# Attention masks added in PSUM by TensorE instead of multiplied in by VectorE, with exp writing the attention tiles and VectorE copying the selected v

## The chip, the core and the metric

The kernel runs on one core of one Trainium2 chip. The metric is the device time of one execution in microseconds. Lower is better. Engines are named as in the profile: PE is TensorE's matmul, PEld its weight load, DVE is VectorE, ACT is ScalarE, POOL is GpSimd and SP is SyncE; L315 is line 315 of the kernel before.

## What is computed

Dilated and plain sliding-window attention (8 batches, 8 heads, 576 positions, head size 64), then a soft mixture of experts over all 4608 rows. The reference, cut to what matters:

```python
def _attn_ref(q, k, v):
    scores = scale * np.matmul(q, k.transpose(0, 1, 3, 2))
    rel = pos[:, None] - pos[None, :]
    mask_plain = (rel >= 0) & (rel < 32)
    mask_dil = (rel >= 0) & (rel < 128) & (rel % 4 == 0)
    masks = np.stack([mask_plain if h < H // 2 else mask_dil for h in range(H)], axis=0)
    scores = np.where(masks[None], scores, -1000000000.0)
    attn = np.exp(scores - np.max(scores, axis=-1, keepdims=True))
    attn = attn / (np.sum(attn, axis=-1, keepdims=True) + 1e-09)
    return np.matmul(attn, v).astype(np.float32)

def _moe_ref(x, phi, w1, w2):       # x: 4608 x 512, 32 slots, 8 experts of 512 -> 1024 -> 512
    logits = x @ phi
    d = softmax of logits over the rows;  slot_input = d.T @ x
    slot_out[e] = np.maximum(slot_input[e] @ w1[e], 0) @ w2[e]
    c = softmax of logits over the slots; return c @ slot_out
```

## The kernel before

A *unit* is one pair of heads of one batch: 32 units, four to a batch, in the order plain, dilated, plain, dilated (`unit`). Heads 0 to 3 are plain and heads 4 to 7 dilated. For each unit the kernel does these stages:

- `transposes`: q and k, loaded with positions on the partitions, are transposed by PE into a ring of two PSUM buffers (L275 for plain heads, L290 for dilated ones), and copied out to qT and kT (ACT at L280; for dilated heads ACT copies q and DVE copies k at L295).
- `scores`: PE multiplies kT by qT (L315). Only blocks of 128 keys against the 160 queries that can see them are computed. A unit has two score tiles (`part` 0 and 1) of two PSUM banks each, one bank for each head. The two heads sit in rows 0 to 63 and 64 to 127 of the array, so each score matmul fills 64 rows. The pool `ps_s`, with the tag `s`, holds two such tiles.
- `softmax_parts`: ACT takes exp of a score tile into fp16 scratch (`pr` at L332, `pd` at L344), and DVE multiplies by a 0/1 mask into the attention tiles: `Pp` for plain heads (L335, three instructions for each unit), `P1` and `P2` for dilated ones (L353, L360). No maximum is subtracted.
- `values`: PE multiplies the attention tiles by v with a column of ones (L395). In a plain unit a block of 128 queries takes a matmul of its own keys and one with the keys of the block before; `Pp` is padded to 256 columns and so all 18 matmuls have 128 output rows. In a dilated unit there are eight such matmuls and sixteen with 32 output rows for the last 16 positions of each residue. DVE takes the reciprocal of the sums and scales (L399, L400).
- `x_transposes` (L416) turns the result for the logits; `front_logits`, `front_rows` and `front_slots` do the softmax over rows and the slot sums of a batch.

v needs a selection for plain heads: `select_v` multiplies v by 0/1 matrices on PE (L205, L216, L225) into two tiles of `ps_s` and one of the ring, once for each batch. ACT copies the three results to `vp` (L213, L234).

The loop at the end of attention emits, for unit u: the scores of u+1, the values of u, the exp and mask of u+1, the transposes of u+3, and parts of the front of the batch before. A scheduler orders the instructions of PE, DVE and ACT from that; POOL's instructions, which are the loads, keep the written order. Each engine executes its list in order and waits by semaphores.

Eight buffers `home0` to `home7` hold first the q, k and v of batch b and later the weights of expert b. POOL issues all loads of q, k and v first, then for each expert w1 (L239) and w2 (L250), where w1 of expert e waits until the transposes of batch e have read home e. After attention, `last_early` and `last_slots` finish the slots of the last batch, `siT` (L654) is made, the experts run in pairs (`expert_in`, L675; `expert_out`, L699), `so` is copied out (L716), and the output phase multiplies (L735), scales on ACT and DVE (L739, L741) and writes (L745, L747).

Of the kernel before, what the change touches and what calls it, by code (L numbers as in the profile page):

```python
# [18 lines left out]
D = 64  # L19
# [17 lines left out]
DW = CL + 16  # L37
OUT_TILES = [(0, 2), (256, 2)] + [(512 + 512 * i, 4) for i in range(7)] + [(4096, 2), (4352, 2)]
# [18 lines left out]
def kernel(  # L57
# [17 lines left out]
    mask = consts.tile([128, QW + 2 * N_SLOTS + 256], FP16, name="mask")  # L75
# [7 lines left out]
    nc.sync.dma_start(out=mask[:, 0 : QW + 64], in_=band_dram.ap())  # L83
# [40 lines left out]
    nc.vector.memset(Pp[:, :, :, QW:], 0.0)  # L124

    nc.vector.memset(Pp[:, :, 4, 64:QW], 0.0)
    nc.vector.memset(Pp[0:1, :, 4, 64:128], 1.0)
    nc.vector.memset(P2, 0.0)
    nc.vector.memset(P2[0:1, :, :, 0, 16:32], 1.0)
    for i in range(2):  # L130
        nc.vector.memset(vd[i][:, :, D : D + 1], 1.0)
# [6 lines left out]
    raw_pool = ctx.enter_context(tc.tile_pool(name="praw", bufs=2))  # L138
    small = ctx.enter_context(tc.tile_pool(name="small", bufs=2))
    x_pool = ctx.enter_context(tc.tile_pool(name="x", bufs=2))  # L140
    dil_pool = ctx.enter_context(tc.tile_pool(name="draw", bufs=2))
# [158 lines left out]
    def scores(u):  # L300
        b, hp = unit(u)
        qT, kT = qTs[u], kTs[u]
        tiles = []
        for part in range(2):
            st = ps_s.tile([128, 2, 512], FP32, name=f"s{u}_{part}", tag="s")
            if hp < 2:
                todo = [(160 * i, 128 * i, 128 * i, QW) for i in range(3)] if part == 0 else [
                    (0, 384, 384, QW), (QW, 512, 512, 64)]
            else:
                todo = [(DW * cc, CL * (2 * cc + part), CL * (2 * cc + part), CL) for cc in range(2)]  # L310
                todo += [(DW * cc + CL, None, CL * (2 * cc + part) + 128, 16) for cc in range(2)]
            for at, k0, q0, n in todo:
                for g in range(2):
                    ks = q0 - 32 * g - 64 * (at // DW) if k0 is None else k0
                    nc.tensor.matmul(  # L315
                        st[:, g, at : at + n],
                        kT[64 * g : 64 * g + 64, ks : ks + 128],
                        qT[64 * g : 64 * g + 64, q0 : q0 + n],
                        start=True,
                        stop=True,  # L320
                    )
            tiles.append(st)
        return tiles

    def softmax_parts(u, tiles):
        b, hp = unit(u)
        for part in range(2):
            st = tiles[part]
            if hp < 2:
                n = (480, 224)[part]  # L330
                pr = raw_pool.tile([128, 2, n], FP16, name=f"pr{u}_{part}", tag=f"pr{part}")
                nc.scalar.activation(out=pr, in_=st[:, :, 0:n], func=AF.Exp, scale=SCALE)  # L332
                for b0, nb, w in ((0, 3, QW),) if part == 0 else ((3, 1, QW), (4, 1, 64)):
                    at = (b0 - 3 * part) * QW
                    nc.vector.tensor_tensor(  # L335
                        out=Pp[:, :, b0 : b0 + nb, 0:w],
                        in0=pr[:, :, at : at + nb * w].rearrange("p h (t c) -> p h t c", c=w),
                        in1=mask[:, None, None, 0:w].broadcast_to([128, 2, nb, w]),
                        op=ALU.mult,
                    )  # L340
                continue
            if part == 0:
                pr = dil_pool.tile([128, 2, 2, 2, DW], FP16, name=f"pd{u}", tag="pd")
            nc.scalar.activation(  # L344
                out=pr[:, part].rearrange("p c e t -> p e c t"),
                in_=st[:, :, 0 : 2 * DW].rearrange("p e (c t) -> p e c t", c=2),
                func=AF.Exp,
                scale=SCALE,
            )
        if hp < 2:  # L350
            return
        pr = pr.rearrange("p a c e t -> p a (c e) t")
        nc.vector.tensor_tensor(  # L353
            out=P1.rearrange("p a c t -> p (a c) t"),
            in0=pr[:, :, :, 0:128].rearrange("p a c t -> p (a c) t"),
            in1=mask[:, None, 0:128].broadcast_to([128, 8, 128]),
            op=ALU.mult,
        )

        nc.vector.tensor_tensor(  # L360
            out=P2.rearrange("p a c s t -> p (a c) s t")[:, :, :, 0:16],
            in0=pr[:, :, :, 128:DW].rearrange("p a c (s t) -> p (a c) s t", s=2),
            in1=mask[:, QW + 64 :].rearrange("p (c s t) -> p c s t", c=8, s=2),
            op=ALU.mult,
        )

    def values(u):
# [7 lines left out]
        for half in range(2):  # L375
# [3 lines left out]
            mms = []  # L379
            for i, blk in enumerate(blocks):  # L380
                for h in range(2):
                    if plain:
                        P, vt = Pp, vp[b % NV]
# [3 lines left out]
                    elif blk < 4:  # L387
                        mms.append((ot[:, i, h], P1[:, h, blk, :], vd[b % 2][:, 4 * (hl + h) + blk, :]))
                    else:
                        for s in range(2):  # L390
                            for c in range(4):
                                vt = vp[b % NV][:, 5, hl + h] if s else vd[b % 2][:, 4 * (hl + h) + c]
                                mms.append((ot[32 * c : 32 * c + 32, i, h], P2[:, h, c, s], vt))
# [109 lines left out]
    def last_early(last):  # L503
# [4 lines left out]
        for dc in range(4):  # L508
# [10 lines left out]
            lr[:, 8:10].rearrange("p i s -> p (i s)"), ident, mask[:, QW : QW + 64],  # L519
# [44 lines left out]
    def spread_masks():  # L564
        sides = mask[:, QW + 64 :].rearrange("p (a c s t) -> p a c s t", a=2, c=4, s=2)
        nc.vector.tensor_copy(
            out=sides[:, :, :, 0].rearrange("p a c t -> p (a c) t"),
            in_=mask[:, None, 128:CL].broadcast_to([128, 8, 16]),
        )
        nc.vector.tensor_copy(  # L570
            out=sides[:, :, :, 1],
            in_=mask[:, QW : QW + 64].rearrange("p (c t) -> p c t", c=4)[:, None].broadcast_to([128, 2, 4, 16]),
        )
        shut = mask[:, QW : QW + 64]
# [206 lines left out]
```

## Time and profile before

| what | value |
|---|---|
| median of 3 runs | 185.55 us (184.9 to 186.19) |
| span of the profiled execution | 183.5 us; no time of its own outside the span is given |
| mean granted TensorE clock over the span | 0.932 |
| PE, PEld busy | 151.8 us (83%), 105.8 us (58%) |
| DVE, ACT, POOL busy | 117.1 us (64%), 115.5 us (63%), 46.9 us (26%) |
| HBM read and written | 62.02 MB, 9.44 MB |
| queue of POOL's loads (q0) | 30.79 MB, 93.9% of 16 DMA engines |
| mask products on DVE (L335, L353, L360) | 16.4 us x48, 10.8 us x16, 4.5 us x16 |
| copies of selected v on ACT (L213, L234) | 9.4 us x16, 4.7 us x8 |
| score matmuls on PE (L315) | 128 of 160 columns, 32 of 64, 128 of 144, 128 of 16 |

The span runs from the first instruction to the last. Busy shares are averages over stages with different limits: attention fills the first 145 us, the experts follow to 157 us, and then the output is written. A wait given for an engine names what came last by the semaphores. Ends of matmuls are modelled, so a busy PE is not a PE at its peak; start-to-start distances are measured.

### The profile page before, as it was taken

Reading aid. Unit: us, or ns where it says so; the run is one execution under the profiler, and the core shown is the slowest. Engines: PE = TensorE matmul, PEld = TensorE weight load, DVE = VectorE, ACT = ScalarE, POOL = GpSimd, SP = SyncE. Lnnn points to the kernel's source line nnn. Section 1 sums busy time; section 2 is a strip of 40 time slices with the busy share of each in tenths; the row PEclk is TensorE's granted clock in tenths of the full one; section 3 lists DMA queues with packets and bytes.
Section 4 is the critical chain, followed back from the end, with each engine's and each line's share of the span. In section 5 each row is a group of like instructions: output and inputs, shape, how many; then the busy total and the mean of one; then the engine's idle time right before and its main releaser. Section 6 shows DMA issues by size and latency. Waiting matters only on the chain.

```text
span 183.5 us, 6054 instructions
## 1 busy us (share of the span) xinstructions
PE 151.8 (83%) x2595; PEld 105.8 (58%) x2595; DVE 117.1 (64%) x363; ACT 115.5 (63%) x208; POOL 46.9 (26%) x77
## 2 busy tenths in 40 slices
PE   1869999999988989998997998898979998885300
PEld 1637776677676667666765767666768644432000
DVE  7605886388877877878779687786970111496410
ACT  2248845689599789779878959977703022675410
POOL 7752555464554654401102001003100000000000
PEclk9999999999999999999999999999995589998555
DMA  5999999999999999999999999999999995199996
GB/s 103 183 203 203 202 203 201 202 202 204 204 201 201 204 199 204 226 211 221 212 216 216 212 216 216 218 212 218 218 214 220 212 208 105 75 440 427 427 427 262
DMA packets 23978, 41.06 MB, mean 224 GB/s; under 512 B 1680, under 2 KB 20240, under 8 KB 21136
## 3 DMA queue, kind: packets, MB, share of 16 engines
q0 software_dynamic: 21584, 30.79, 93.9%
q1 hardware_dynamic: 2368, 9.89, 13.4%
q8 instruction: 20, 0.33, 0.6%
q14 instruction: 6, 0.05, 0.1%
HBM read 62.02 MB, written 9.44 MB: 389 GB/s over the span
## 4 chain that ended last, share of the span: by engine, by line
DMA 74%; issue 15%; POOL 3%; ACT 2%; DVE 1%; PE 0%; POOLq 0%; DVEq 0%; SPq 0%
DMA home<-in_moe_w_dram 31%; DMA home<-in_v_dram 15%; DMA home<-in_k_dram 12%; DMA home<-in_q_dram 9%; DMA out_dram<-ot 7%; ACT ot L739 2%; DVE ot L741 1%; POOL home L250 1%; POOL home L162 1%; POOL home L239 1%; POOL home L184 0%; POOL home L187 0%; ACT so L716 0%; PE sop L699 0%; PE f L735 0%
## 5 line engine op out<-in xcount | busy, mean ns | idle before, releaser
L400 DVE TENSOR_TENSOR x<-o,rc 128x384 f16<-128x384 f32 x64 | 29.9, 482 | 0.5
L332 ACT ACTIVATE pr<-s 128x960 f16<-128x960 f32 (+1 forms) x32 | 24.7, 780 | 1.8 <-PE s L315 1.8
L344 ACT ACTIVATE pd<-s 128x640 f16<-128x640 f32 x32 | 20.9, 706 | 1.7 <-PE s L315 1.7
L162 POOL DMA_DIRECT2D home<-in_v_dram x24 | 16.6, 692 | 16.6 <-DMA home<-in_k_dram 11.6
L205 PE MATMUL sel<-home,pick 32*128 32x256 f16 x128 | 17.8, 307 | 1.4 <-DMA home<-in_v_dram 1.1
L399 DVE RECIPROCAL rc<-o 128x6 f32<-128x6 f32 x64 | 10.2, 177 | 13.5 <-PE o L395 13.4
L416 PE MATMUL rgx<-ident,x 128*128 128x128 f16 x160 | 15.6, 233 | 3.0 <-ACT qT L295 3.0
L741 DVE TENSOR_SCALAR ot<-f,rrow 128x512 f32<-128x512 f32 (+1 forms) x19 | 12.5, 716 | 7.7 <-DMA out_dram<-ot 5.2
L335 DVE TENSOR_TENSOR Pp<-pr,mask 128x960 f16<-128x960 f16 (+2 forms) x48 | 16.4, 394 | 0.4 <-ACT pr L332 0.4
L280 ACT COPY qT<-rgq 128x576 f16<-128x576 f16 x16 | 10.3, 641 | 9.0 <-PE rgq L275 8.5
L422 ACT COPY xT<-rgx 128x512 f16<-128x512 f16 x16 | 9.6, 601 | 10.0 <-PE rgx L416 10.0
L739 ACT ACTIVATE ot<-f,rrow 128x512 f32<-128x512 f32 (+1 forms) x19 | 11.2, 675 | 7.0 <-DMA out_dram<-ot 6.6
L239 POOL DMA_DIRECT2D home<-in_moe_w_dram x8 | 4.3, 534 | 44.4 <-PE rgq L290 36.5
L213 ACT CAST vp<-sel 128x512 f16<-128x512 f32 x16 | 9.4, 590 | 9.2 <-PE sel L205 9.0
L416 PEld LDWEIGHTS <-x 128*128 128x128 f16 x160 | 10.2, 102 | 7.2 <-issue 5.4
L735 PE MATMUL f<-so,ET 128*128 128x512 f16 (+1 forms) x38 | 11.0, 402 | 3.9 <-ACT ot L739 3.0
L275 PEld LDWEIGHTS <-home 96*64 96x64 f16 x384 | 11.9, 123 | 3.9 <-issue 2.0
L184 POOL DMA_DIRECT2D home<-in_k_dram x16 | 10.6, 661 | 10.1 <-DMA home<-in_q_dram 8.2
L395 PE MATMUL o<-vp,Pp 128*128 128x65 f16 x288 | 12.9, 203 | 0.0
L436 PE MATMUL l<-xT,phi 128*128 128x288 f16 x64 | 10.8, 304 | 2.0 <-ACT qT L280 1.7
L295 DVE COPY kTd<-rgk 128x576 f16<-128x576 f16 x16 | 12.0, 752 | 0.6 <-PE rgk L290 0.5
L295 ACT COPY qT<-rgq 128x576 f16<-128x576 f16 x16 | 10.3, 646 | 3.1 <-PE rgq L290 2.6
(105 smaller groups left out, 292.9 us busy)
## 6 DMA issues: line engine op xcount, KB each, us to landing
home<-in_moe_w_dram POOLq DMA_DIRECT2D x15, 1024.0 KB, 30.1
out_dram<-ot SPq DMA_DIRECT2D x7, 1024.0 KB, 7.5
home<-in_k_dram POOLq DMA_DIRECT2D x16, 288.0 KB, 9.9
home<-in_q_dram POOLq DMA_DIRECT2D x15, 288.0 KB, 9.7
home<-in_v_dram POOLq DMA_DIRECT2D x16, 256.0 KB, 9.8
out_dram<-ot SPq DMA_DIRECT2D x3, 512.0 KB, 6.5
home<-in_moe_w_dram POOLq DMA_DIRECT2D x2, 512.0 KB, 27.3
home<-in_v_dram POOLq DMA_DIRECT2D x8, 64.0 KB, 8.9
```

The costliest lines, as they stand in the source:

```text
L162: nc.gpsimd.dma_start(out=dst, in_=v[b, h0 : h0 + n_h, r0 : r0 + 4 * n_p, :].rearrange("h (p r) d -> p h (r d)", r=4),)
L205: nc.tensor.matmul(sel[:, n, 0], pick[rows, r].rearrange("p i j -> p (i j)"), raw[rows, :, r, :], start=(r == 0), stop=(r == 3), tile_posi ...
L275: nc.tensor.transpose(rg[64 * h : 64 * h + 64, r, :], raw[:, 2 * hp + h, D * r : D * r + D], ident[0:NP, 0:NP],)
L295: (nc.scalar.copy if nm == "q" else nc.vector.tensor_copy)(out=dst[:, 0:S].rearrange("c (g p a) -> c g p a", g=4, a=3), in_=rg.rearrange(" ...
L332: nc.scalar.activation(out=pr, in_=st[:, :, 0:n], func=AF.Exp, scale=SCALE)
L335: nc.vector.tensor_tensor(out=Pp[:, :, b0 : b0 + nb, 0:w], in0=pr[:, :, at : at + nb * w].rearrange("p h (t c) -> p h t c", c=w), in1=mask ...
L344: nc.scalar.activation(out=pr[:, part].rearrange("p c e t -> p e c t"), in_=st[:, :, 0 : 2 * DW].rearrange("p e (c t) -> p e c t", c=2), f ...
L395: nc.tensor.matmul(to, lhs, rhs, start=(n == 0), stop=(n == len(mms) - 1), skip_group_check=True)
L400: nc.vector.tensor_tensor(out=x[:, blocks[0] : blocks[0] + nb, D * hl : D * hl + 2 * D].rearrange("p t (h d) -> p t h d", h=2), in0=ot[:, ...
L416: nc.tensor.transpose(rg[:, 128 * blk : 128 * blk + 128], x[:, blk, hl : hl + 128], ident)
L739: nc.scalar.activation(out=ot[:, j, d0:d1], in_=fp, func=AF.Copy, scale=scale)
L741: nc.vector.tensor_scalar(out=ot[:, j, d0:d1], in0=fp, scalar1=scale, scalar2=None, op0=ALU.mult)
```

## The change

The mask becomes a number that is added. `constants` gives 0 where a key may be seen and -60000 where not. For each score tile and head, PE first multiplies the identity by the mask into PSUM (`start=True`), and the scores are added on top (`start=False`). ACT's exp then writes straight into the attention tiles, of which there are now two of each kind (`Pp`, `Pd`), used in turn. The scratch tiles, the mask products on DVE and the zero padding of `Pp` go. In `values`, a plain block's matmul with the keys of the block before now has 32 output rows instead of 128, and the order in each half is first the matmuls with 128 output rows, then those with 32. The sixteen short matmuls of a dilated unit, which went through four residues with one operand and then with the other, take both operands of a residue in turn. The three copies of the selected v move from ACT to DVE. The tile `shut`, used once for the last batch, gets its own buffer, and `spread_masks` spreads the dilated mask into `mask_d`.

The diff, cut to its core:

```diff
-    keep = ((d >= 0) & (d < WINDOW)).astype(np.float16)
+    keep = (d >= 0) & (d < WINDOW)
...
-    band = np.concatenate([keep, ends], axis=1).astype(np.float16)
+    band = np.where(np.concatenate([keep, ends], axis=1), 0.0, MASKED).astype(np.float16)
...
-    Pp = kept([128, 2, NKB, 256], "Pp")
-    P1 = kept([128, 2, 4, 128], "P1")
-    P2 = kept([128, 2, 4, 2, 32], "P2")
+    Pp = [kept([128, 2, PW], f"Pp{i}") for i in range(2)]
+    Pd = [kept([128, 8 * DW + 16], f"Pd{i}") for i in range(2)]
+    shut = kept([128, 2 * N_SLOTS], "shut")
+    mask_d = kept([128, 2, 2, DW], "mask_d")
...
-            nc.scalar.copy(out=vp[b % NV][:, 2 * i : 2 * i + 2, :, 0:D], in_=sel[:, :, 0])
+            nc.vector.tensor_copy(out=vp[b % NV][:, 2 * i : 2 * i + 2, :, 0:D], in_=sel[:, :, 0])
...
-        nc.scalar.copy(out=vp[b % NV][:, 4:6, :, 0:D], in_=end)
+        nc.vector.tensor_copy(out=vp[b % NV][:, 4:6, :, 0:D], in_=end)
...
             st = ps_s.tile([128, 2, 512], FP32, name=f"s{u}_{part}", tag="s")
+            for g in range(2):
+                if hp >= 2:
+                    to, shut_out = st[:, g, 0 : 2 * DW], mask_d[:, g].rearrange("p c t -> p (c t)")
+                elif part == 0:
+                    to = st[:, g, 0 : 3 * QW].rearrange("p (t c) -> p t c", t=3)
+                    shut_out = mask[:, None, 0:QW].broadcast_to([128, 3, QW])
+                else:
+                    to, shut_out = st[:, g, 0 : QW + 64], mask
+                nc.tensor.matmul(
+                    to, ident, shut_out, start=True, stop=False, skip_group_check=True
+                )
...
+            for n, (to, lhs, rhs) in enumerate(mms):
+                nc.tensor.matmul(
+                    to, lhs, rhs, start=False, stop=(n >= len(mms) - 2), skip_group_check=True
+                )
...
-                nc.scalar.activation(out=pr, in_=st[:, :, 0:n], func=AF.Exp, scale=SCALE)
-                for b0, nb, w in ((0, 3, QW),) if part == 0 else ((3, 1, QW), (4, 1, 64)):
-                    at = (b0 - 3 * part) * QW
-                    nc.vector.tensor_tensor(
...
+                a, z = ((0, 480), (480, 704))[part]
+                to, frm = Pp[u // 2 % 2][:, :, a:z], st[:, :, 0 : z - a]
+            else:
+                to = Pd[u // 2 % 2][:, 4 * DW * part : 4 * DW * part + 4 * DW].rearrange(
+                    "p (c e t) -> p e c t", c=2, e=2
+                )
+                frm = st[:, :, 0 : 2 * DW].rearrange("p e (c t) -> p e c t", c=2)
+            nc.scalar.activation(out=to, in_=frm, func=AF.Exp, scale=SCALE)
...
-                        mms.append((ot[:, i, h], P[:, h, blk, 0:128], vt[:, blk, hl + h, :]))
+                        mms.append((ot[:, i, h], P[:, h, QW * blk : QW * blk + 128], vt[:, blk, hl + h, :]))
                         if blk > 0:
-                            mms.append((ot[:, i, h], P[:, h, blk - 1, 128:256], vt[:, blk - 1, hl + h, :]))
...
+                            ends.append((
+                                ot[0:32, i, h], P[:, h, QW * blk - 32 : QW * blk], vt[:, blk - 1, hl + h, :]
+                            ))
...
+                    for c in range(4):
+                        z = DW * c + 128
+                        to = ot[32 * c : 32 * c + 32, i, h]
+                        ends.append((to, P[:, z : z + 32], vt[:, 4 * (hl + h) + c, :]))
+                        ends.append((to, P[:, z + 16 : z + 48], vp[b % NV][:, 5, hl + h, :]))
+            mms += ends
```

More of the change, by code (lines that the diff above doesn't have):

```diff
@@ L37 @@
 DW = CL + 16
+PW = 768
 OUT_TILES = [(0, 2), (256, 2)] + [(512 + 512 * i, 4) for i in range(7)] + [(4096, 2), (4352, 2)]
@@ L74 @@
     ident = consts.tile([128, 128], FP16, name="ident")
-    mask = consts.tile([128, QW + 2 * N_SLOTS + 256], FP16, name="mask")
+    mask = consts.tile([128, QW + 64], FP16, name="mask")
     phi_sb = consts.tile([128, 4, N_SLOTS], FP32, name="phi_sb")
@@ L82 @@
     nc.sync.dma_start(out=ident, in_=ident_dram.ap())
-    nc.sync.dma_start(out=mask[:, 0 : QW + 64], in_=band_dram.ap())
+    nc.sync.dma_start(out=mask, in_=band_dram.ap())
     nc.sync.dma_start(out=phi_sb, in_=moe_phi.rearrange("(p r) s -> p r s", r=4))
@@ L123 @@
     nc.vector.memset(kTd[:, S:], 0.0)
[L124 to L129, printed above, removed]
     for i in range(2):
+        nc.vector.memset(Pp[i][:, :, 704:], 0.0)
+        nc.vector.memset(Pp[i][0:1, :, 704:], 1.0)
+        nc.vector.memset(Pd[i][:, 8 * DW :], 0.0)
         nc.vector.memset(vd[i][:, :, D : D + 1], 1.0)
@@ L137 @@
     qT_pool = ctx.enter_context(tc.tile_pool(name="qT", bufs=2))
-    raw_pool = ctx.enter_context(tc.tile_pool(name="praw", bufs=2))
     small = ctx.enter_context(tc.tile_pool(name="small", bufs=2))
     x_pool = ctx.enter_context(tc.tile_pool(name="x", bufs=2))
-    dil_pool = ctx.enter_context(tc.tile_pool(name="draw", bufs=2))
     big = tc.alloc_tile_pool(name="big", bufs=1)
@@ L305, in scores @@
             st = ps_s.tile([128, 2, 512], FP32, name=f"s{u}_{part}", tag="s")
-            if hp < 2:
-                todo = [(160 * i, 128 * i, 128 * i, QW) for i in range(3)] if part == 0 else [
-                    (0, 384, 384, QW), (QW, 512, 512, 64)]
-            else:
[L310 to L321, printed above, removed]
+            for g in range(2):
[9 more added lines that the diff above has]
+                )
@@ new lines, in scores @@
+            mms = []
+            if hp < 2:
+                todo = [(160 * i, 128 * i, QW) for i in range(3)] if part == 0 else [
+                    (0, 384, QW), (QW, 512, 64)]
+                for at, k0, n in todo:
+                    for g in range(2):
+                        rows = slice(64 * g, 64 * g + 64)
+                        mms.append((st[:, g, at : at + n], kT[rows, k0 : k0 + 128], qT[rows, k0 : k0 + n]))
+            else:
+                for cc in range(2):
+                    q0 = CL * (2 * cc + part)
+                    for g in range(2):
+                        rows = slice(64 * g, 64 * g + 64)
+                        mms.append(
+                            (st[:, g, DW * cc : DW * cc + CL], kT[rows, q0 : q0 + 128], qT[rows, q0 : q0 + CL])
+                        )
+                for cc in range(2):
+                    q0 = CL * (2 * cc + part) + 128
+                    for g in range(2):
+                        rows, k0 = slice(64 * g, 64 * g + 64), q0 - 32 * g - 64 * cc
+                        mms.append((
+                            st[:, g, DW * cc + CL : DW * cc + DW], kT[rows, k0 : k0 + 128], qT[rows, q0 : q0 + 16]
+                        ))
@@ L329, in softmax_parts @@
             if hp < 2:
-                n = (480, 224)[part]
-                pr = raw_pool.tile([128, 2, n], FP16, name=f"pr{u}_{part}", tag=f"pr{part}")
-                nc.scalar.activation(out=pr, in_=st[:, :, 0:n], func=AF.Exp, scale=SCALE)
-                for b0, nb, w in ((0, 3, QW),) if part == 0 else ((3, 1, QW), (4, 1, 64)):
-                    at = (b0 - 3 * part) * QW
-                    nc.vector.tensor_tensor(
[L336 to L365, printed above, removed]
+                a, z = ((0, 480), (480, 704))[part]
[3 more added lines that the diff above has]
+                    "p (c e t) -> p e c t", c=2, e=2
+                )
+                frm = st[:, :, 0 : 2 * DW].rearrange("p e (c t) -> p e c t", c=2)
+            nc.scalar.activation(out=to, in_=frm, func=AF.Exp, scale=SCALE)
     def values(u):
@@ L378, in values @@
             ot = ps_o.tile([128, 3, 2, D + 1], FP32, name=f"o{u}_{half}", tag="o")
-            mms = []
+            mms, ends = [], []
             for i, blk in enumerate(blocks):
@@ L382, in values @@
                     if plain:
-                        P, vt = Pp, vp[b % NV]
-                        mms.append((ot[:, i, h], P[:, h, blk, 0:128], vt[:, blk, hl + h, :]))
+                        P, vt = Pp[u // 2 % 2], vp[b % NV]
+                        mms.append((ot[:, i, h], P[:, h, QW * blk : QW * blk + 128], vt[:, blk, hl + h, :]))
                         if blk > 0:
-                            mms.append((ot[:, i, h], P[:, h, blk - 1, 128:256], vt[:, blk - 1, hl + h, :]))
[L387 to L393, printed above, removed]
+                            ends.append((
+                                ot[0:32, i, h], P[:, h, QW * blk - 32 : QW * blk], vt[:, blk - 1, hl + h, :]
+                            ))
+                        continue
+                    P, vt = Pd[u // 2 % 2][:, 4 * DW * h :], vd[b % 2]
+                    if blk < 4:
+                        mms.append((ot[:, i, h], P[:, DW * blk : DW * blk + 128], vt[:, 4 * (hl + h) + blk, :]))
+                        continue
+                    for c in range(4):
[4 more added lines that the diff above has]
+            mms += ends
             for n, (to, lhs, rhs) in enumerate(mms):
@@ L518, in last_early @@
         nc.tensor.matmul(
-            lr[:, 8:10].rearrange("p i s -> p (i s)"), ident, mask[:, QW : QW + 64],
+            lr[:, 8:10].rearrange("p i s -> p (i s)"), ident, shut,
             start=True, stop=False, skip_group_check=True,
@@ L564, in spread_masks @@
     def spread_masks():
-        sides = mask[:, QW + 64 :].rearrange("p (a c s t) -> p a c s t", a=2, c=4, s=2)
         nc.vector.tensor_copy(
-            out=sides[:, :, :, 0].rearrange("p a c t -> p (a c) t"),
-            in_=mask[:, None, 128:CL].broadcast_to([128, 8, 16]),
+            out=mask_d[:, :, :, CL:],
+            in_=mask[:, QW:].rearrange("p (c e t) -> p e c t", c=2, e=2),
         )
         nc.vector.tensor_copy(
-            out=sides[:, :, :, 1],
-            in_=mask[:, QW : QW + 64].rearrange("p (c t) -> p c t", c=4)[:, None].broadcast_to([128, 2, 4, 16]),
+            out=mask_d[:, :, :, 0:CL].rearrange("p e c t -> p (e c) t"),
+            in_=mask[:, None, 0:CL].broadcast_to([128, 4, CL]),
         )
-        shut = mask[:, QW : QW + 64]
+        nc.vector.tensor_copy(out=mask[:, QW:], in_=mask[:, 0:64])
         nc.vector.memset(shut[:, 0:N_SLOTS], 0.0)
```

## The prediction

> **What bounds the kernel now.** I read the chain of waits first, then the stretch of the timeline in which the last weights are asked for and used, then the table of windows, and last the PE timeline of one batch.
>
> The chain of waits (start, length, what):
>
> ```profile
> 73.18 28.81 DMA home<-in_moe_w_dram
> ...
> 128.48 28.27 DMA home<-in_moe_w_dram
> 156.74 0.04 issue
> 156.78 0.42 PE sop L699 x4
> 157.21 0.02 issue
> 157.23 0.59 ACT so L716
> ```
>
> The chain is transfers from 4 to 156.7 us, then the output. Read alone it says that no compute engine matters. The timeline round the end of the chain says otherwise:
>
> ```profile
> 111.96 0.53 POOL L239 DMA_DIRECT2D home<-in_moe_w_dram  x1 [13.75 <-PE rgq L290]
> 126.91 0.53 POOL L239 DMA_DIRECT2D home<-in_moe_w_dram  x1 [14.42 <-PE rgq L290]
> ...
> 144.24 0.29 DVE L654 TENSOR_TENSOR siT<-last,rtot 128x128 f16<-128x128 f32 x1
> ...
> 155.47 1.72 PE L699 MATMUL sop<-home,hTp 128*32 128x512 f16 x23
> ...
> 156.79 0.10 PEld L699 LDWEIGHTS <-hTp 128*32 128x32 f16 x3 [0.44 <-issue]
> ```
>
> The experts begin when siT is there (144.53) and run without a stall on weights until their last four matmuls, which wait 0.44 us for the transfer that lands at 156.74. So two chains end within half a microsecond of each other: the weights, and attention -> siT -> experts. Attention made faster gains at most those last instants, for the transfers still land at 156.74. Attention made slower by X moves the end by X - 0.4. (The weights have slack: the request at 126.91 lands at 146.95, 4.9 us of that its own transfer, so it could come 15 us later without the queue running dry.)
>
> The table of windows (length; then busy time and count of PE, PEld, DVE, ACT, POOL; clock, DMA share, GB/s):
>
> ```profile
> 15.11:18.53 3.42, 3.42 (x68) 2.96 (x65) 1.52 (x7) 2.92 (x6) 0.67 (x1) 1.00 1.35 204
> ...
> 75.00:90.00 15.00, 13.81 (x294) 10.25 (x291) 12.12 (x38) 12.53 (x24) 2.12 (x4) 1.00 1.05 218
> 105.00:120.00 15.00, 13.80 (x294) 10.27 (x291) 12.12 (x38) 12.53 (x24) 0.53 (x1) 1.00 1.04 217
> ```
>
> From 39 us on every batch takes 14.95 us (the two POOL rows above are one batch apart), whatever the transfers do: attention is paced by its engines, PE first with 13.8.
>
> The PE timeline of one stretch:
>
> ```profile
> 110.86 0.72 PE L395 MATMUL o<-vp,Pp 128*128 128x65 f16 x18
> 111.42 0.42 PE L290 MATMUL rgq<-ident,home 96*128 96x96 f16 x6
> 111.67 0.42 PE L290 MATMUL rgk<-ident,home 96*128 96x96 f16 x6
> 112.02 0.38 PE L315 MATMUL s<-qT,kTp 64*128 64x160 f16 x6
> 112.91 0.44 PE L416 MATMUL rgx<-ident,x 128*128 128x128 f16 x5 [0.51 <-ACT qT L295]
> ```
>
> Two things are to be seen. Six transposes take 0.25 us when the next group uses the whole array too (111.42 to 111.67), and 0.35 when it is the 64-row score matmuls (111.67 to 112.02). Start to start, this batch has 33 such changes of tile shape (whole array, 64 rows, 32 rows, 32 columns), each about 95 ns. And there are four real stalls, beyond streaming 0.67 (the one shown), 0.33, 0.43 and 0.37 us; less the 0.095 of the change in each, 1.42 us. So PE's own work is 14.95 - 1.42 = 13.53 us a batch.
>
> **The change, part by part.**
>
> *Masks on PE, added.* Every score tile gets two whole-array matmuls ahead of its scores: 480 and 224 columns for each of two heads in a plain unit, four of 320 in a dilated one. A batch has two units of each: 2 x 1408 + 2 x 1280 = 5376 columns. The 288-column logits (L436) start 122 ns apart, 0.423 ns a column: 2.27 us a batch. The scores themselves still run.
>
> *Tile shapes.* Each tile now goes whole array -> 64 rows, and back for the next mask; and the overlap of a plain block with the one before is now a 32-column matmul, in groups of four behind groups of whole-array ones, where L395 had 18 alike (0.56 us, no change). Against that, the new instruction order breaks up the v selection less. Counted in the built order of a steady batch: 42 changes instead of 33, +9 x 0.095 = 0.86 us.
>
> *The 32-column tails.* Before, four neighbours used four different column groups and started 3 ns apart; now two or four in a row use the same one. No row shows that. From below 29 ns each, as whole-array L395 in a row: nothing more. From above a drained 95 ns for each that follows its own column group, 6 a plain unit and 8 a dilated one: 28 x 0.095 = 2.7 us a batch. I take 0, since L395, the nearest row, reloads the same array at 29 ns; 2.7 is a rival.
>
> *Removed from DVE.* A batch loses 2 x (646 + 319 + 219) + 2 x (676 + 282) ns of mask products (L335, L353, L360) and gains three PSUM copies at L596's 684 ns: 12.12 - 4.28 + 2.05 = 9.9 us. ACT loses 3 x 588 ns: 10.8 us. Both were within PE's shadow and get deeper into it, so I cost both at nothing. On DVE the copies stand behind U_sb (0.69) and xT (0.45), and the buffer they free is awaited by the next dilated mask; that comes only after the rest of the selection (some 1.5 us of PE), which covers the 0.68. In the first batch they queue behind vd, which waits for v until 14.04; the mask that needs the buffer comes about 16, the copy ends near 15.9: even. The setup copies of the masks run near 6 us, 7 us ahead of the first scores. SP and POOL issue the same transfers in the same order.
>
> *The stalls.* The mask matmul stands ahead of scores and of the x transposes on PE's queue and waits for the exp of the tile two before; that exp ends some 0.3 us sooner than PE arrives. While ACT copies qT it gives PE 0.4 us of work where PE stood still. Between 0 and 1.42 us of stalls can remain; I take 0.3, for PE now comes later to everything.
>
> Steady batch: 13.53 + 2.27 + 0.86 + 0.3 = 17.0 us, 2.0 more. From 39.0 to 134.5 there are 95.5 / 14.95 = 6.4 batches: **+12.8 us**.
>
> *The first 39 us.* The profile reports clock 1.00 here, but the matmuls say half: 18 L395 take 1.17 us at 17.46 and at 35.80, then 0.72. From first scores (13.3) to 39 us that is 1.40 batches at 18.34 us each (17.46 to 35.80); the same work at full pace would be 10.3 us (13.53 less 3.2 of logits, rows and slots that come later), a ratio of 1.78. Added at full pace: 2.27 + 14 changes x 0.095 = 3.6 us a batch, 5.05 in all. If the pace doubles at time t, the position of 39.0 is reached at t + 14.4 + 5.05 - (t - 13.3) / 1.78: at 44.1 for t = 39, 35.1 for t = 18.5. When will it double? Clock records lie on a grid of 3.41 us. Weighing each matmul by the rows and columns it fills, the last slow window (35.59 to 39.01) filled 3186 of 4096 half-pace cycles; no earlier one passed 3042; 144.82 to 148.23, which ended the second slow stretch, had 3460. Whole-array masks fill more: by the order of the new kernel I find the first window near 3100 about 25.4 to 28.8, so t = 28.8, reached at 39.6: **+0.6**.
>
> The Trainium skill ("TensorE: Matmul & The Clock Gate", Part 1) says that one busy window of some 3.4 us brings the full clock. This trace disagrees: in 15.11:18.53 PE is busy 3.42 of 3.42 us, and it stays slow for 20 us more. By the page t would be 18.5.
>
> *The end.* At 133.69 PE waits 0.87 us for the last mask product; that wait goes: **-0.9**. The experts now begin at another point of the 3.41 us grid; before, the slow stretch ended one window after they began (145.03 to 148.23), and up to 3.4 us more at half pace would cost 1.7: I take **+0.8**. Slack **-0.4**. The output phase stays.
>
> Sum: 12.8 + 0.6 - 0.9 + 0.8 - 0.4 = 12.9. The profiled execution spans 183.5 us, so 196.4; the median of the runs, 185.55, lies 2.0 above the span, so **198.5 us**.
>
> **The rivals.**
>
> *PE is not the pace, ACT is* (not slower). ACT's 12.53 us and its waits of 2.3 a batch also fill 14.95. If the 95 ns gaps are waits that overlap, PE's work is the sum of median gaps, 11.0 us a batch, and 13.3 with masks; ACT, 1.8 us lighter, then sets a pace below 14.95, and the weights at 156.74 hold the end: 185.5. It decides where PE's work stays under 14.95. Against it: the gaps appear just where the shape changes, also with operands long there.
>
> *The clock rises at once*, t = 18.5: 35.1 instead of 39.6, 4.5 less: 194.0. For it: dense masks. Against it: the windows above. The clock page's rule ends here.
>
> *The clock stays low until 39 us*: 44.1, 4.5 more: 203.0. For it: missed fills of 2897 and 3042 before.
>
> *Tails drain each other*: 2.7 us in 7.8 batches, 21 more: 219.5.
>
> **How the numbers follow.** Forecast 0.45 (196 to 201 with stalls of 0 to 0.7 a batch), clock at once 0.23, clock late 0.15, ACT's pace 0.10, draining tails 0.07. The range leaves out the last two: 191 (early clock, no stall: 0.3 x 6.4 = 1.9 less, and the grid's 0.8) to 206 (late clock, stalls of 0.8). Within 1% is what a measurement here can't tell from no change; ACT's pace gives 0.08 there and, were the last wait to shrink too, 0.02 faster. Slower 0.90.
>
> **What would show it.** Steps are right if w1 requests late in POOL's timeline lie about 17.0 us apart, if six L287 transposes ahead of whole-array masks take 0.25 us, if a mask matmul of 480 columns takes PE 0.20, if the chain of waits runs through PE and ACT instead of weights before 170 us, and if DVE and ACT are idle more, waiting for PE. The forecast is wrong if the batch stays at 15 us, if plain tails start 100 ns apart, or if L392 paces change at another window than 25 to 32 us.

## The result, and the profile after

The changed kernel takes 204.49 us (203.96 to 204.84), against 185.55 before: a ratio of 1.101, 95% interval 1.098 to 1.105. It is slower by 18.9 us; 198.5 was forecast, with a range to 206. The profiled execution spans 203.1 us. Here and below, executions of a kernel that took over 1.5% longer than its fastest are left out of the ratios and their intervals, but not of the medians.

The chain of waits no longer runs on transfers through attention. These are pieces of it from one batch and from the end (start, length, what):

```profile
89.60 0.97 PE o L392 x18
91.03 0.65 ACT qT L292
92.97 0.60 PE o L392 x24
94.75 1.18 PE l L433 x8
...
148.02 17.10 DMA home<-in_moe_w_dram
165.12 1.76 PE h L671 x18
...
174.26 1.43 PE sop L695 x23
175.72 0.59 ACT so L712
```

By engine the page gives the chain 41% PE and 19% DMA, where it was 74% DMA. PE's work and the copies of qT that it waits for carry attention; what carries the end is the experts' matmuls. The chain names a landing of weights at 165.12 us ahead of them, but siT is done at 165.05, 0.07 earlier, and the matmuls that start then are those of the first experts, whose weights were asked for first. Experiment 4 separates the two.

The POOL timeline shows the requests of the last experts' weights:

```profile
108.59 0.53 POOL L236 DMA_DIRECT2D home<-in_moe_w_dram  x1 [16.48 <-DVE rc L396]
109.11 0.54 POOL L247 DMA_DIRECT2D home<-in_moe_w_dram  x1
126.12 0.53 POOL L236 DMA_DIRECT2D home<-in_moe_w_dram  x1 [16.47 <-PE rgq L287]
146.46 0.53 POOL L236 DMA_DIRECT2D home<-in_moe_w_dram  x1 [19.81 <-PE rgq L287]
```

Before, such requests were 14.95 us apart. Here the first two w1 rows are 17.53 apart and the last two 20.34. The last request comes 19.5 us later than before, more than the 15 us of slack that the transfers had.

The table of windows, with the columns as before (length; busy time and count of PE, PEld, DVE, ACT, POOL; clock, DMA share, GB/s):

```profile
75.00:90.00 15.00, 14.58 (x270) 9.79 (x268) 9.01 (x24) 9.76 (x19) 1.06 (x2) 1.00 1.06 218
105.00:120.00 15.00, 14.71 (x258) 9.75 (x257) 8.87 (x25) 9.81 (x18) 1.05 (x2) 1.00 1.03 216
135.00:150.00 15.00, 14.38 (x214) 9.03 (x211) 8.64 (x23) 7.42 (x13) 2.12 (x4) 0.77 0.42 74
```

In 15 us PE is now busy for 14.6 instead of 13.8; DVE falls from 12.1 to 9.0 and ACT from 12.5 to 9.8. They have become idler and the batch longer. The last row has two other things: the transfers stand still for part of it (share 0.42), and the granted clock is 0.77. Its records say half clock from 139.0 to 145.8.

One stretch of the PE timeline:

```profile
107.06 1.04 PE L392 MATMUL o<-vp,Pp 128*128 128x65 f16 x18
108.04 0.43 PE L287 MATMUL rgq<-ident,home 96*128 96x96 f16 x6
108.30 0.42 PE L287 MATMUL rgk<-ident,home 96*128 96x96 f16 x6
108.56 0.57 PE L311 MATMUL s<-mask,ident 128*128 128x480 f16 x2
109.25 0.44 PE L413 MATMUL rgx<-ident,x 128*128 128x128 f16 x5
109.62 0.38 PE L338 MATMUL s<-qT,kTp 64*128 64x160 f16 x6
109.93 0.37 PE L311 MATMUL s<-mask,ident 128*128 128x224 f16 x2
110.23 0.27 PE L338 MATMUL s<-qT,kTp 64*128 64x160 f16 x4
```

The 18 matmuls of plain values take 0.98 us to the next group (0.56 before): four changes between 128 and 32 columns. The transposes ahead of a whole-array mask take 0.26, without the tenth that a change of shape cost. The two masks of 480 columns stream 0.41 us from 108.56, yet the next group starts at 109.25: 0.28 us are lost there, for the transposes of x need a ring buffer that ACT is still copying out of:

```profile
108.56 0.64 ACT L292 COPY qT<-rgq 128x576 f16<-128x576 f16 x1 [0.69 <-PE rgq L287]
```

Where the span's 19.5 us went, by the starts and ends of the same work in both traces:

| stretch | before, us | after, us | difference |
|---|---|---|---|
| start to the first scaling of unit 4 | 36.56 | 37.61 | +1.05 |
| units 4 to 24, five batches | 74.81 | 87.60 | +12.8 |
| units 24 to 28, one batch | 14.95 | 20.13 | +5.2 |
| unit 28 to the end of siT | 18.21 | 19.71 | +1.5 |
| siT to the start of so | 12.70 | 10.67 | -2.0 |
| so to the end | 26.32 | 27.35 | +1.0 |

### The profile page after: what moved, and what is told of

Read it like the earlier page. It is cut to its first block, busy times and chain, and to the rows that moved or that the text cites. A ratio compares the mean times of both kernels' runs of the same rounds, so it can differ in the third digit from the quotient of the medians.

```text
span 203.1 us, 6199 instructions
## 1 busy us (share of the span) xinstructions
PE 174.7 (86%) x2723; PEld 112.0 (55%) x2723; DVE 108.4 (53%) x309; ACT 104.7 (52%) x184; POOL 46.8 (23%) x77
## 4 chain that ended last, share of the span: by engine, by line
PE 41%; issue 19%; DMA 19%; ACT 8%; DVE 5%; POOL 3%; ACTq 0%; POOLq 0%; DVEq 0%; SPq 0%
DMA home<-in_moe_w_dram 8%; PE o L392 8%; PE s L338 7%; PE s L311 7%; DMA out_dram<-ot 7%; DMA home<-in_k_dram 4%; PE rgx L413 3%; ACT qT L292 3%; PE l L433 2%; PE rgq L272 2%; PE h L671 2%; PE rgq L287 2%; ACT qT L277 2%; ACT ot L735 2%; PE sop L695 1%
## 5 line engine op out<-in xcount | busy, mean ns | idle before, releaser
L356 ACT ACTIVATE Pd<-s 128x640 f16<-128x640 f32 x32 | 21.7, 703 | 22.3 <-PE s L338 22.3
L356 ACT ACTIVATE Pp<-s 128x960 f16<-128x960 f32 (+1 forms) x32 | 22.7, 763 | 4.7 <-PE s L338 4.6
L396 DVE RECIPROCAL rc<-o 128x6 f32<-128x6 f32 x64 | 11.8, 184 | 23.2 <-PE o L392 23.2
L159 POOL DMA_DIRECT2D home<-in_v_dram x24 | 16.6, 692 | 17.7 <-DMA home<-in_k_dram 10.1
L392 PE MATMUL o<-vp,Pp 128*128 128x65 f16 (+1 forms) x288 | 17.7, 202 | 0.0
L292 ACT COPY qT<-rgq 128x576 f16<-128x576 f16 x16 | 10.2, 638 | 14.0 <-PE rgq L287 14.0
L737 DVE TENSOR_SCALAR ot<-f,rrow 128x512 f32<-128x512 f32 (+1 forms) x19 | 12.5, 717 | 8.6 <-DMA out_dram<-ot 6.3
L311 PE MATMUL s<-mask,ident 128*128 128x480 f16 (+1 forms) x64 | 16.2, 337 | 0.0
L311 PE MATMUL s<-mask_d,ident 128*128 128x320 f16 x64 | 15.4, 323 | 0.3
L338 PEld LDWEIGHTS <-kTd 64*128 64x128 f16 x256 | 9.0, 98 | 11.6 <-issue 10.8
L277 ACT COPY qT<-rgq 128x576 f16<-128x576 f16 x16 | 10.2, 638 | 9.1 <-PE rgq L272 8.5
L392 PEld LDWEIGHTS <-Pp 128*128 128x128 f16 (+1 forms) x288 | 12.8, 100 | 3.2
L292 DVE COPY kTd<-rgk 128x576 f16<-128x576 f16 x16 | 12.1, 757 | 3.9 <-PE rgk L287 3.9
L338 PE MATMUL s<-qT,kTd 64*128 64x144 f16 (+1 forms) x256 | 14.0, 205 | 0.0
L338 PE MATMUL s<-qT,kTp 64*128 64x160 f16 (+1 forms) x160 | 13.9, 238 | 0.0
```

The lines of the kernel that those rows point to most:

```text
L159: nc.gpsimd.dma_start(out=dst, in_=v[b, h0 : h0 + n_h, r0 : r0 + 4 * n_p, :].rearrange("h (p r) d -> p h (r d)", r=4),)
L277: nc.scalar.copy(out=dst[:, 0:S].rearrange("c (p r) -> c p r", r=RP), in_=rg.rearrange("c r p -> c p r"),)
L292: (nc.scalar.copy if nm == "q" else nc.vector.tensor_copy)(out=dst[:, 0:S].rearrange("c (g p a) -> c g p a", g=4, a=3), in_=rg.rearrange(" ...
L311: nc.tensor.matmul(to, ident, shut_out, start=True, stop=False, skip_group_check=True)
L338: nc.tensor.matmul(to, lhs, rhs, start=False, stop=(n >= len(mms) - 2), skip_group_check=True)
L356: nc.scalar.activation(out=to, in_=frm, func=AF.Exp, scale=SCALE)
```

## The experiments

**Theory.** PE's own work sets the pace of a batch: the columns of the masks are the larger term, and about 95 ns for each change of tile shape the other. DVE and ACT don't matter, and the weights only cap what a faster attention could gain. **Rivals:** the gaps at changes of shape are waits that overlap, and ACT is the pace; the v copies, now on DVE, hold the next mask; the late weights hold the end. The period of a batch is read from the starts of the first scaling (L396 in the changed kernel) of every fourth unit, in the middle of attention. In the changed kernel it repeats there within 0.02 us. It is 14.95 us before (14.85 to 15.13) and 17.53 after.

| kernel | changes of shape a batch | batch, us | median, us | ratio to before (95%) |
|---|---|---|---|---|
| changed | 42 | 17.53 | 204.49 | 1.101 (1.098 to 1.105) |
| 1: masks first | 29 | 16.76 | 198.52 | 1.069 (1.063 to 1.075) |
| 2: whole tails | 34 | 16.67 | 196.93 | 1.058 (1.053 to 1.063) |
| 3: no masks | 45 | 15.66 | 196.54 | 1.042 (1.036 to 1.048) |
| 4: spare w1 | 42 | 17.53 | 204.54 | 1.102 (1.099 to 1.104) |
| 5: both orders | 21 | 16.09 | 192.18 | 1.038 (1.033 to 1.044) |
| 6: masks twice | 37 | 19.30 | 215.07 | 1.160 (1.156 to 1.163) |
| 7: v copies on ACT | 42 | 17.42 | 202.49 | no interval |
| 8: before, no products | 32 | 14.64 | 186.0 | 1.001 (0.999 to 1.003) |
| 9: longer warm-up | 42 | 17.53 | 203.93 | 1.085 (1.074 to 1.095) |

The runs of 3 go from 192.8 to 199.78 us and those of 9 from 201.53 to 206.01.

### 1. Masks of both tiles first

```diff
             for g in range(2):
...
                 nc.tensor.matmul(to, ident, shut_out, start=True, stop=False, ...)
+            tiles.append(st)
+        for part in range(2):
+            st = tiles[part]
             mms = []
```

> The changed kernel, with the masks of both score tiles of a unit issued ahead of the scores of both. The same matmuls, in another order: by count of the built order a steady batch has 29 changes of tile shape on PE instead of 42. If each change costs PE 95 ns that nothing hides, a batch falls from 17.53 to about 16.3 us and the time by 13 x 0.095 x 7.8 batches = 9.6 us, to about 195. If the gaps at changes of shape are waits that overlap with others, the time stays at 204.

The batch fell by 0.77 us, not 1.24. The direction is the theory's; the rest came back as waits. PE's waits from 60 to 120 us (in total, times, longest):

```profile
PE u L488 <- ACT qT L277: 0.8, 4, 0.2
PE s L311 <- DVE vp L210: 0.7, 4, 0.2
PE l L435 <- ACT qT L277: 0.6, 3, 0.2
```

In the changed kernel only the first of these three is listed:

```profile
PE u L486 <- ACT qT L277: 0.6, 3, 0.2
```

The second is new: the mask of the second tile now comes so early that the selected v hasn't left its buffer. These rows count idle time only after the modelled end of a matmul. From start to start the second costs 0.33 us a batch beyond streaming, and the third 0.35 where the changed kernel has 0.07. That is 0.6 us more, which covers the missing 0.47 and leaves about 0.15 that I can't place.

### 2. Plain tails on the whole array again

```diff
-    Pp = [kept([128, 2, PW], f"Pp{i}") for i in range(2)]
+    Pp = [kept([128, 2, NKB, 256], f"Pp{i}") for i in range(2)]
...
-                            ends.append((
-                                ot[0:32, i, h], P[:, h, QW * blk - 32 : QW * blk], vt[:, blk - 1, hl + h, :]
-                            ))
+                            mms.append((ot[:, i, h], P[:, h, blk - 1, 128:256], vt[:, blk - 1, hl + h, :]))
```

> The changed kernel, with the tails of plain heads as matmuls with 128 output rows again, from attention tiles padded with zeros (ACT writes a plain unit in three instructions instead of two). 34 changes of shape in a steady batch instead of 42, the same count of matmuls. At 95 ns each: batch 16.8 us, time 5.9 us less, 198.6. If the tails are as dear by reloading their own column group, more: down to 2.7 us a batch, 184 to 190. If neither matters: 204.

The batch fell by 0.86 us with eight changes fewer: 107 ns each, the count of matmuls being the same. The 18 matmuls take this again:

```profile
93.88 0.72 PE L396 MATMUL o<-vp,Pp 128*128 128x65 f16 x18
```

The padding and the third exp instruction on ACT cost nothing that shows. The step to 32 columns saved nothing: a matmul that follows another starts 36 ns behind it (median in the changed kernel) with 32 columns and 34.5 with 128. After a change of shape the first starts of a group are 35 to 39 ns apart instead of 29, whatever the columns, which is about what 107 has over 95. So the tails don't drain each other either, which was the dearest of the rivals.

### 3. No mask matmuls (masking left out)

```diff
-                nc.tensor.matmul(to, ident, shut_out, start=True, stop=False, skip_group_check=True)
...
-                    to, lhs, rhs, start=False, stop=(n >= len(mms) - 2), skip_group_check=True
+                    to, lhs, rhs, start=True, stop=True
```

> The changed kernel without the mask matmuls; it leaves the masking out. The scheduler then interleaves more: 45 changes of shape in a steady batch instead of 42. If PE's streaming of 5376 mask columns is the larger term, a batch falls by 2.27 - 0.28 to about 15.5 us and the time to about 189. If ACT sets the pace, lighter by 1.8 us than before, the batch falls to 13 to 14 us and the weights hold the end at 185.

The batch is 15.66 us, where 15.5 was expected: masks less three changes are worth 1.87. Without masks it is still longer than before, with ACT 1.8 us lighter, so ACT isn't the pace. The median, though, is far above the 189 that the batch would give. The windows of the profiled run (198.66 us) say why for that run:

```profile
75.00:90.00 15.00, 14.47 (x280) 10.45 (x279) 9.90 (x28) 10.17 (x21) 2.21 (x5) 1.00 1.05 217
120.00:135.00 15.00, 14.79 (x224) 10.08 (x223) 7.26 (x22) 9.02 (x18) 0.53 (x1) 0.66 1.03 216
```

Without the masks the full clock came only at 48.3 us, and it was lost again for 10.2 us from 120. The batch in that stretch took 19.16 us. The two shorter runs, 192.8 and 194.42 us, left no profile; they lie above 189 too, and what held them is open.

### 4. The last w1 in memory of its own

```diff
+    spare = big.tile([128, 4096], FP16, name="spare", tag="spare")
...
-        w1t = t[:, 0:4096].rearrange("p (c f) -> p c f", c=4)
+        w1t = (spare if e == 7 else t[:, 0:4096]).rearrange("p (c f) -> p c f", c=4)
```

> The changed kernel, with the first weights of the last expert loaded into memory of their own, so that they needn't wait for the transposes of the last batch. The transfers then have work while they stood still in the changed kernel (some 11 us from 135 us on). If attention and the experts behind it are what ends last, the time stays at 204 (within 1). If the late weights hold the end, it falls by 5 or more. A third reading: the clock drop at 139 us in the changed kernel goes with the quiet of the transfers; then the drop is gone and some 2.6 us with it.

The weights now land by 155.8 us instead of 164.8, and the time doesn't move (204.54). So the late weights don't hold the end. (In the changed kernel the transfers stood still for 7 us, from 140.6 to 147.7, and not for the 11 that were expected.) In this profile the clock isn't lost at 139 us and the last batch takes 17.83 us, but the experts run at half clock at their start (siT to so 11.8 us instead of 10.7). Whether it was the busier queue or the other phase of the clock's windows, one profile can't say.

### 5. Both orders at once

This kernel has the edits of 1 and 2.

> Both orders at once: masks of both tiles first, and plain tails with 128 output rows. 21 changes of shape in a steady batch instead of 42. If the changes cost 95 ns each and add up: batch 15.5 us, time 15.6 us less than the changed kernel, about 189. If they hide each other or a stall takes their place, not below 194.

16.09 us: 1.44 less, of the 1.63 that 1 and 2 gave by themselves and the 2.0 expected. The changes of shape add up, but from about 16 us on other waits show:

```profile
99.97 0.42 PE L288 MATMUL rgq<-ident,home 96*128 96x96 f16 x6
100.23 0.42 PE L288 MATMUL rgk<-ident,home 96*128 96x96 f16 x6
100.49 0.57 PE L312 MATMUL s<-mask,ident 128*128 128x480 f16 x2
101.23 0.44 PE L419 MATMUL rgx<-ident,x 128*128 128x128 f16 x5 [0.18 <-ACT qT L293]
```

The wait for the copy of qT, one of the real stalls before the change, costs 0.34 us here, where the changed kernel had 0.28. The larger new ones are the two of experiment 1, 0.33 and 0.40 us. The time, 192.18 us, is the best of the kernels that mask in PSUM, and still above before.

### 6. Every mask matmul twice

```diff
-                nc.tensor.matmul(to, ident, shut_out, start=True, stop=False, ...)
+                for n in range(2):
+                    nc.tensor.matmul(to, ident, shut_out, start=(n == 0), stop=False, ...)
```

> The changed kernel with each mask matmul issued twice (the sum of two masks shuts out as well). 5376 more columns a batch of the same shape as their neighbours, and 37 changes of shape instead of 42. If PE is the pace: +2.27 - 0.48 = +1.8 us a batch, 19.3 us, and some 14 us in all: 218. If the masks run in PE's waits: 204 to 207.

19.30 us a batch, as expected: +1.77 with five changes fewer. At 0.095 each that makes 2.25 us for 5376 columns, against 2.27 from the logits' row. The masks hide behind nothing.

### 7. The copies of v back on ACT

```diff
-            nc.vector.tensor_copy(out=vp[b % NV][:, 2 * i : 2 * i + 2, :, 0:D], in_=sel[:, :, 0])
+            nc.scalar.copy(out=vp[b % NV][:, 2 * i : 2 * i + 2, :, 0:D], in_=sel[:, :, 0])
```

> The changed kernel with the copies of the selected v back on ACT. DVE 2.05 us a batch lighter, ACT 1.8 us heavier. If neither engine is on the path: 204, within 1. If the copies on DVE stand behind others and hold the next mask: 2 to 5 us less.

The batch is 17.42 us, 0.11 shorter. In the changed kernel the dilated mask behind the selection of v starts 0.13 us late; here it doesn't. So that tenth is what the copies cost on DVE, and neither engine sets the pace. The median is 2 us lower. In its profile the clock isn't lost at 139 us, and the last batch takes 17.70 instead of 20.13, which is more than the difference. Its runs go from 198.8 (mean clock 0.959) to 202.96 (0.933), so I read no more than the batch from it.

### 8. The kernel before, without the mask products

The products on DVE are taken out and the values use constant attention tiles; the masking and the scores' part in the values are left out.

> The kernel before without the mask products on DVE; the values then use constant attention tiles, so the masking and the use of the scores in the values are left out. Attention gets faster (no wait on DVE's products, batch 14 to 14.9 us), and the time stays within 0.5 of 185.5 if the last weights, landing at about 156.7, hold the end. If attention holds the end, the time falls with it by 1 to 5 us.

The batch is 14.64 us and siT is ready at 142.30 us instead of 144.54. The time is the same, within 0.3% of before. The last matmuls of the experts wait for what the attention gained:

```profile
156.29 0.40 PE L679 MATMUL sop<-home,hTp 128*32 128x512 f16 x4 [1.43 <-DMA home<-in_moe_w_dram]
```

They begin at 156.29; in the kernel before the same four began at 156.78. A faster attention gains 0.5 us and then waits for weights, as read from the profile before. So while the transfers stay as they are, no version of this edit could have gained more.

### 9. A longer warm-up

```diff
-    warm(6, ring, "ring")
+    warm(14, ring, "ring")
```

> The changed kernel with 56 whole-array matmuls ahead of everything instead of 24 (from 4.0 to about 10 us instead of 7.5), which fills at least one whole window of 3.41 us. If one window filled by whole-array matmuls brings the full clock, it comes before 12 us instead of 26.4, provided the gaps up to 14 us don't take it away again, and the first four units are done some 3 to 5 us earlier, less up to 2.6 us by which the first transposes start later: 200 to 203. If a filled window isn't what counts, the clock rises about 26 us as before and the time is 204 to 207.

The records give full clock from 13.2 us, half again from 16.6, and full from 26.9. These are three windows on the clock's grid, with the columns as before:

```profile
6.38:9.80 3.42, 3.42 (x22) 2.26 (x21) 2.88 (x18) 0.00 (x0) 1.79 (x3) 1.00 1.32 199
9.80:13.21 3.41, 3.41 (x51) 3.06 (x52) 0.00 (x0) 0.56 (x2) 1.81 (x3) 1.00 1.27 201
13.21:16.62 3.41, 2.44 (x34) 1.31 (x26) 2.08 (x4) 1.25 (x3) 2.03 (x3) 1.00 1.34 203
```

The first holds only whole-array matmuls and shows PE busy throughout. But some of them start 232 ns apart, where the others start 107 ns apart, and counted as in the prediction it is filled to 2560 of 4096 cycles. It didn't bring the full clock. The second, filled to 3552, did. So no window was filled whole, and the full clock came later than the 12 us expected. In the third PE waits, for 0.97 us of it here, and the full clock is lost:

```profile
15.62 0.56 PE L311 MATMUL s<-mask,ident 128*128 128x480 f16 x2 [0.97 <-DVE vp L210]
```

Unit 4 came at 38.66 us instead of 37.61, since the first transposes started 4.5 us late. In this profile, of a run of 204.9 us, nothing was gained. The other runs took 201.53, 202.95 and 206.01 us, with mean clocks of 0.942, 0.935 and 0.903; what the two shorter ones gained, and by what, no profile shows.

## Why the prediction was right, and which terms were off

**The bound.** Right. Two chains that end together, with the weights as the floor: shown by 8 (faster attention, same time) and by 4 (earlier weights, same time). The weights' slack of 15 us was overrun: the last request came 19.5 us later, the queue stood still for 7 us, and the last transfer ended at 164.8 us instead of 156.4. That didn't matter, as the experts are later still.

**Masks on PE, 2.27 us.** Right: 2.25 by experiment 6.

**Tile shapes, 0.86 us.** Right in kind and about in size: 107 ns for each in 2, 95 by the gaps. It also was the part of the change that could have been had for less: 2 undoes it in the plain tails and 1 in the masks. The Trainium skill ("TensorEngine Tiling (Array Packing)", Key Properties) says that switching the tiling mode drains TensorE; the trace agrees, and gives the price.

**The 32-column tails, nothing.** Right: 36 ns against 34.5.

**DVE and ACT, nothing.** Right to 0.1 us a batch: 7 gets back the 0.13 us that a mask waited for the copies on DVE.

**The stalls, 0.3 us.** This is the term that was mis-sized most. Between 0 and 1.42 I took 0.3, since PE would come later to everything. Beyond streaming and the change of shape, a batch of the changed kernel has 0.28 and 0.28 us after the 480-column masks, 0.27 and 0.10 round the slot matmuls, 0.13 after the selection and 0.06 before the logits: 1.1 us. The ring of two buffers is why: its next user on PE waits for ACT's copy however long PE's list has become, and the mask between them covers 0.41 us of it and no more. That is read from the traces; no run has a larger ring. The terms then make 17.76 for 17.53 measured. Of the 0.23 over, 0.10 is counted twice, for the kernel before waits as long at its slot matmuls and the 13.53 holds that; the rest I can't place. Over 6.4 batches the difference of 0.53 is 3.4 us.

**The first 39 us, +0.6.** Measured +1.05 by unit 4 and +0.66 two scalings later, where the kernel before is at 40.1 us, and the clock rose at 26.4 us, inside the 25.4 to 28.8 of the forecast. But the rule behind it, 3100 of 4096 filled cycles, fell. Counted in the same way, the window that ended at 26.4 us had 2652, and earlier ones with 3028 and 2924 had not done it. Over all runs the windows that brought the clock go from 2380 to 3712 and those that didn't reach 3172. That the sum came out is luck as well: with the rise at 26.4, where 28.8 was taken, the same formula gives -0.5, so more than 1 us was lost elsewhere in this stretch. What holds is the direction, for lasting full clock: 48.3 us without masks, 39.0 before, 21.4 to 26.9 in the kernels with masks once, 19.7 with masks twice. Kernel 8, without masks in PSUM, had it at 22.0, lost it at 32.2 and had it again from 42.5.

**The end, -0.9 + 0.8 - 0.4.** The experts gained 2.0 us, for they found the clock full where I took the middle of the grid and a loss of 0.8. The output phase cost 1.0 more, which I had at nothing. It is 27.3 to 27.4 us in the changed kernel and all its variants but 7 (26.7), and 26.3 in the kernel before and in 8. The chains have the difference in the writes of the output: the two on the path take 3.98 and 8.43 us before, and 4.18 and 9.34 in the changed kernel. Why the same writes take longer I haven't found.

**Missed altogether:** the half clock from 139.0 to 145.8 us in the last full batch, 2.6 us. It wasn't the quiet of the transfers: they came to rest only at 140.6 us, and 6 and 7 have transfers at rest too, and keep the full clock until 169.9 and 154.4 us. The window ahead of it had a fill of 3136 of 8192, and others with 2752 kept the clock. What takes it away is open.

The sum for the span was 12.9 us and 19.5 were measured. Of the 6.6 between them, 3.4 are from stalls, 2.6 from the clock, 1.0 from the output and 0.45 from the start. The experts gave back 2.4 (2.0 gained where a loss of 0.4 was forecast), and about 1.6 these don't place. The two large misses, the lost clock and the experts, nearly cancel. That 204.49 still lies inside the range is partly luck: its upper end was made of a late clock, which didn't come, and of stalls of 0.8, which came to 1.1, while the lost clock and the longer writes were in none of its terms.

## What to carry to other kernels

A chain of waits that is all transfers doesn't make the engines free: look at what stands ready just before the chain's last link, and how long it has been waiting. Moving work from an engine that is 80% busy to one that paces the batch costs its full price, and on TensorE every switch between whole-array, row-tiled and column-tiled matmuls is to be counted along with the columns. Put matmuls of one shape together, and keep short ones at the full shape if they stand between full ones: 32 columns instead of 128 saved nothing here and cost about 107 ns for each switch.

## What the runs showed of the hardware that wasn't expected

- Matmuls with 96 and 128 rows follow each other without a gap; 64 rows, 32 rows or 32 columns after them cost about 95 ns at full clock, and as much on the way back.
- The clock of TensorE changes in steps of 3.41 us and follows how full the array is, more than whether PE counts as busy. PE was busy for 3.42 of 3.42 us in a window of the kernel before that stayed at half. Without masks the full clock was lost for 10.2 us in mid-attention, after a window in which PE is shown busy for 3.32 of 3.41 us. Counted as in the prediction, over all eleven profiles, every half-clock window filled to more than 3172 of 4096 cycles was followed by full clock; no full-clock window filled to more than 3136 of 8192 was followed by half, and none below 2684 by full. Between 2380 and 3172 at half clock, and between 2684 and 3136 at full, both happened. The Trainium skill ("TensorE: Matmul & The Clock Gate", Part 1) gives one busy window as the condition for full clock. These traces don't agree: neither that window of attention nor the one of run 9 that holds whole-array matmuls alone, busy for 3.42 of 3.42 us, brought it.
